# Local values of two runs as one operation on four tiles of TensorE, and narrow products split into 32 columns

## The chip, the cores and the metric

The kernel runs on one core of one Trainium2 chip. The metric is the device time of one execution in microseconds (us). It was run three times before the change: 905.56, 905.9 and 907.25 us, the median is 905.9 us.

## The reference

Attention with 4 batches, 8 heads, 576 tokens and head size 64, followed by two feed-forward layers on 2304 tokens of width 512 with inner width 2048. All is fp32. Cut to what matters:

```python
q_d, k_d, v_d = (x.reshape(B, H, S // 4, 4, D).mean(axis=3) for x in (q, k, v))
out_up = np.repeat(softmax(q_d @ k_d.T / 8) @ v_d, 4, axis=2)       # pooled over four tokens
mask = np.abs(pos[:, None] - pos[None, :]) < 4
out_local = softmax(np.where(mask, q @ k.T / 8, -1e9)) @ v          # seven neighbours
x = (out_up + out_local).transpose(0, 2, 1, 3).reshape(2304, 512)
h = x @ w_in;  x = np.where(h > 0, h, np.exp(np.minimum(h, 0)) - 1) @ w_out
h = x @ w2_in; out = (s * np.maximum(h, 0) ** 2 + b) @ w2_out
```

## The kernel before, in words

Attention is worked in units: one batch and one pair of heads (16 units, `hp` is the pair). A unit has a pooled part and a local part.

The pooled part: `tr` (L678) transposes q and k on TensorE, copies them to SBUF as `T` (scaled for q) and sums groups of four tokens out of PSUM with a reduction on VectorE (L689) to give `d`. `gs` (L702) multiplies the sums to pooled scores: for each head a matmul that loads 72 columns (a half of 144 pooled queries) and moves 144 pooled keys. After a softmax `gpt_` (L748) transposes the weights, and `gpv` (L767) multiplies with the summed values `vd`: for each head and half of the keys a matmul that loads 64 columns and moves 72 or 144.

The local part exists so in the first two batches alone (`DIRECT = 2`; the other two work it on VectorE and GpSimd in `direct`). The tokens of a half (288) are nine blocks of 32 queries; a block sees 38 keys. `ls` (L788) makes the scores of both heads, 18 matmuls that load 32 columns and move 38, into a PSUM tile for each head. `softmax` (L810) leaves weights for both heads in one buffer `p`; `lpt_` (L853) transposes it, so that head 0 stands on partitions 0 to 37 and head 1 on 64 to 101. `lpv` (L866) multiplies with the windows of v: 18 matmuls that load 64 columns (38 rows) and move 32, head 0 in the first 64 rows and 64 columns of the array, head 1 in the last, into one PSUM tile. Its result and the pooled one are added (L880), split into a high and a low fp32r part (`split`, L897) and used as input of the first feed-forward layer, or stored for later.

The first batch runs in two stages: `attention0` with the first half of the tokens before any feed-forward product, `attention0_rest` with the second half beside the first products. The second batch (`attention`) runs both halves of each unit beside feed-forward products. `ffn_h` (L1040) and `ffn_x` (L1086) are the first layer, with 256 columns moved by each matmul; lines 1474, 1502 and 1572 the second layer, which the change does not touch.

The order on every engine comes from a planner. Each operation is given an engine, an estimated duration, what it reads and writes, and a due time; `Plan.emit` runs a simulated clock over all of them and issues, for each engine, the ready operation with the earliest due time. A hand-tuned table `SHIFT` adds or takes away from the due times of operations by their number. Where TensorE would be idle in the plan `fill` puts in matmuls of zeros (L1635, source `wz`); before an operation that is not feed-forward, up to the planned time `DENSE_TILL`, `thicken` puts some in too when the planned feed-forward work just before it is below `DENSE`. Loads go through SP's queue, with a planned transfer time of bytes times `slow`. PSUM has three rings of tiles: `at` (2), `h` (2) and `acc` (4); a ring's next tile waits until its last user is done. Softmax buffers `p` are two, `pt` three.

Of the kernel before, what the change touches and what calls it, by code (L numbers as in the profile page):

```python
# [99 lines left out]
class Plan:  # L100
# [11 lines left out]
    SHIFT = ((29, 33, -0.5), (124, 125, 4.5), (127, 131, -22), (172, 178, -5), (212, 218, 11), (220, 226, 17.5),  # L112
# [9 lines left out]
    ENTER = 4.0  # L122
    DENSE = 0.9
    DENSE_TILL = 45.0
# [226 lines left out]
def attn_moe_moe2(ctx, tc, q, k, v, w_in, w_out, w2_in, w2_out, s2, b2, mask, mask_d, out):  # L351
# [32 lines left out]
    for tag, n, size in (("raw", 2, 8192), ("ev", 2, 2048), ("xr", 2, 2048), ("r", 2, 1024), ("wu", 2, 3584), ("pt", 3, 1152),  # L384
                         ("p", NLP, 1536), ("gnm", 2, 16), ("lmx", 2, 24), ("lrs", 2, 24), ("gs4", 2, 16), ("grs", 2, 16),
                         ("dmx", 2, 16), ("dsm", 2, 16)):
        ar.place(tag, n, size, "work")
# [29 lines left out]
             "lsm": [p1.tile([QB, 2 * NQB, 2], F32, name=f"lsm{i}") for i in range(2)],  # L417
# [69 lines left out]
    def weights(ph, f):  # L487
# [9 lines left out]
        for i in range(2):  # L497
# [9 lines left out]
            load(rawp[i], 524288, ld, due - RL, u=[raw])  # L507
# [37 lines left out]
    class Unit:  # L545
        def __init__(self, b, hp):
# [38 lines left out]
            self.gp, self.gpt, self.lp, self.lpt = {}, {}, {}, {}  # L585

# [5 lines left out]
        def loads(self, due, late=0, nb=0.0, nb_late=0.0):  # L592
# [9 lines left out]
            def parts(i, n0, n1, late):  # L602
                for a in range(2):
# [3 lines left out]
                         due + (late if late else 0), u=[self.nat], slow=1.2, nb=nb + (nb_late if late else 0), queue=e)  # L607
# [13 lines left out]
            load(self.vg, 294912, vg, due + VO, u=self.both if b == 0 else (), nb=nb)  # L621

            def vw(half, a):

                n, o = NQB * CT, a * D
                at = (2 * hp + a + b * H) * S + half * HS - 3
                dst = self.vw(half)
# [8 lines left out]
            def loads_v(half):  # L636
                for a in range(2):
                    load(self.vwp[half], VR * NQB * CT * 256, lambda a=a: vw(half, a),
                         due + VO + (late if half else 0), r=[self.vd] if b == 0 and half else (), u=self.both,
                         n=3 if (b, hp, a, half) == (0, 0, 0, 0) else 1, slow=1.2, nb=nb + (nb_late if half else 0))  # L640
# [37 lines left out]
        def tr(self, i, half, due):  # L678
            ps = self.ps([128, NQB, QB])

            def pe():
                for m in range(NQB):
# [5 lines left out]
                 scale=SCALE if i else 1.0, r=[ps], w=[self.T], u=self.tdv, due=due)  # L688
# [13 lines left out]
        def gs(self, heads, halves, due):  # L702
# [998 lines left out]
```

## Time and profile before

| what | value |
|---|---|
| median of three runs | 905.9 us (905.56 to 907.25) |
| the profiled execution, its own time | 906.92 us |
| its span, first to last instruction | 905.1 us |
| TensorE busy, weight loads busy | 893.3 us, 863.2 us |
| VectorE, ScalarE, GpSimd busy | 703.0, 546.6, 385.3 us |
| mean granted TensorE clock | 0.994 of full |

A busy share says how long an engine had an instruction under way. TensorE's instructions overlap, and the ends of its matmuls are modelled, so the time that a group of them takes is better read from the start of the group to the start of the next. In a timeline, equal instructions that follow each other are one row with their count.

### The profile page before, as it was taken

To read this page: it belongs to the slowest core of one execution; us is meant where nothing else is said; L and a number is where in the kernel's file an instruction comes from. 1 tells how busy PE (TensorE), PEld (TensorE's weight loads), DVE (VectorE), ACT (ScalarE), POOL (GpSimd) and SP (SyncE) were. 2 spreads that over 40 slices of the span, in tenths; PEclk is the share of its full clock that TensorE was granted. 3 is DMA by queue.
4 is the path that set the end of the run, shared out by engine and by line. 5 is a ranking of instruction groups with operands and counts; after the bars stand their busy time and mean duration, and the time that the engine had idled before them with its cause. 6 is when DMAs were issued, how large, how long until landed. Compare 5 with 4: busy or idle time off the path is not lost.

```text
span 905.1 us, 21207 instructions
## 1 busy us (share of the span) xinstructions
PE 893.3 (99%) x8417; PEld 863.2 (95%) x8417; DVE 703.0 (78%) x1090; ACT 546.6 (60%) x1175; POOL 385.3 (43%) x349
## 2 busy tenths in 40 slices
PE   9999999999999999999999999999999999999998
PEld 5678999999999989999999999999999999999998
DVE  5467766798888888889775768999836999677785
ACT  6587767565445545444566675656665887566642
POOL 3656557687887877988536664000000000000000
PEclk9989999999999999999999999999999999999999
DMA  9839676563353453343502156699963884353411
GB/s 188 221 116 237 187 184 172 132 175 92 90 135 80 106 130 105 85 114 101 158 7 94 49 188 215 239 335 342 362 217 120 271 296 150 110 180 104 157 37 35
DMA packets 123524, 142.88 MB, mean 158 GB/s; under 512 B 50976, under 2 KB 93984, under 8 KB 123424
## 3 DMA queue, kind: packets, MB, share of 16 engines
q1 hardware_dynamic: 121632, 141.07, 52.5%
q8 instruction: 66, 1.08, 0.5%
q10 hardware_dynamic: 1792, 0.44, 0.2%
q14 instruction: 34, 0.28, 0.1%
HBM read 101.12 MB, written 40.37 MB: 156 GB/s over the span
## 4 chain that ended last, share of the span: by engine, by line
PE 92%; DVE 2%; DMA 2%; POOL 1%; ACT 1%; issue 1%; SPq 1%; POOLq 0%; ACTq 0%
PE acc L1086 21%; PE h L1040 18%; PE acc L1572 11%; PE acc L1502 10%; PE h L1572 6%; PE h L1502 5%; PE at L1572 3%; PE acc L1040 3%; PE at L1502 3%; PE acc L1474 3%; DMA work<-in_moe_w_out_dram 1%; PE at L874 1%; PE at L775 1%; PE at L1635 1%; PE at L683 1%
## 5 line engine op out<-in xcount | busy, mean ns | idle before, releaser
L1086 PE MATMUL acc<-split,w 128*128 128x256 f32 x1728 | 234.4, 286 | 0.0
L1086 PEld LDWEIGHTS acc<-split,w 128*128 128x128 f32 x1728 | 217.2, 190 | 2.2 <-issue 1.7
L1040 PE MATMUL h<-split,w 128*128 128x256 f32 x1488 | 201.4, 286 | 1.6 <-POOL split L465 1.3
L1040 PEld LDWEIGHTS h<-split,w 128*128 128x128 f32 x1488 | 186.6, 189 | 4.1 <-POOL split L465 1.5
L465 POOL TENSOR_TENSOR split<-work,split 128x256 fp32r<-128x256 f32 (+1 forms) x148 | 138.6, 947 | 71.6 <-ACT split L457 54.9
L1572 PE MATMUL acc<-w,attn 128*128 128x256 f32 x864 | 106.1, 281 | 0.0
L1572 PEld LDWEIGHTS acc<-w,attn 128*128 128x128 f32 x864 | 104.1, 189 | 0.0
L1502 PE MATMUL acc<-attn,w 128*128 128x256 f32 x768 | 99.3, 282 | 0.0
L1502 PEld LDWEIGHTS acc<-attn,w 128*128 128x128 f32 x768 | 95.3, 188 | 0.0
L457 ACT ACTIVATE split<-work 128x256 fp32r<-128x256 f32 (+2 forms) x164 | 67.3, 422 | 45.0 <-DVE work L1064 26.9
L1064 DVE SCALAR_TENSOR_TENSOR work<-work,h 128x256 f32<-128x256 f32 x124 | 50.9, 415 | 55.4 <-ACT work L1062 55.2
L1060 ACT ACTIVATE work<-h 128x256 f32<-128x256 f32 x124 | 46.9, 379 | 75.4 <-PE h L1040 48.7
L465 POOL TENSOR_TENSOR work<-work 128x896 f32<-128x896 f32 (+1 forms) x42 | 69.1, 1652 | 15.9 <-DVE work L847 7.6
L1564 DVE TENSOR_TENSOR attn<-split,attn 128x1024 fp32r<-128x1024 f32 x43 | 52.6, 1223 | 21.5 <-ACT attn L1563 21.1
L1563 ACT ACTIVATE attn<-split 128x1024 fp32r<-128x1024 f32 x43 | 45.2, 1056 | 32.5 <-DVE split L1583 13.9
L982 DVE TENSOR_REDUCE work<-work 128x128 f32<-128x896 f32 x36 | 63.5, 1790 | 1.6 <-POOL work L465 1.6
L1062 ACT ACTIVATE work<-work 128x256 f32<-128x256 f32 x144 | 59.8, 417 | 4.0
L1572 PE MATMUL h<-w,attn 128*128 128x256 f32 x432 | 54.2, 281 | 0.0
L1522 ACT ACTIVATE split<-split 128x512 f32<-128x512 f32 x44 | 27.5, 629 | 41.4 <-DVE split L1512 40.6
L1572 PEld LDWEIGHTS h<-w,attn 128*128 128x128 f32 x432 | 52.5, 189 | 0.0
L1502 PE MATMUL h<-attn,w 128*128 128x256 f32 x384 | 51.2, 282 | 0.0
L1502 PEld LDWEIGHTS h<-attn,w 128*128 128x128 f32 x384 | 48.3, 188 | 0.0
(192 smaller groups left out, 1535.6 us busy)
## 6 DMA issues: line engine op xcount, KB each, us to landing
gd<-split SPq DMA_DIRECT2D x57, 256.0 KB
work<-gd SPq DMA_DIRECT2D x20, 512.0 KB
work<-in_moe_w_in_dram SPq DMA_DIRECT2D x16, 512.0 KB
work<-in_moe_w_out_dram SPq DMA_DIRECT2D x16, 512.0 KB
work<-in_moe_w_in_dram SPq DMA_DIRECT2D x8, 1024.0 KB
work<-in_moe_w_out_dram SPq DMA_DIRECT2D x8, 1024.0 KB
split<-gd SPq DMA_DIRECT2D x16, 512.0 KB
work<-in_k_dram SPq DMA_DIRECT2D x17, 320.0 KB
```

What stands on the lines that cost most here:

```text
L457: a = ((0.07 if first.slot in plan.spare else 0.11) + n / 1200, lambda: nc.scalar.activation(out=out(), in_=src(), func=ACTF.Copy, scale=s ...
L465: f = lambda e: lambda: e.tensor_tensor(out=out(), in0=in0(), in1=in1(), op=alu)
L982: op("dve", 0.07 + 14 * D / 546, lambda: nc.vector.tensor_reduce(out=vo()[:, WD + j * D:WD + (j + 2) * D].rearrange("p (j d) -> p j d", j= ...
L1040: nc.tensor.matmul(ps(), lhsT=w()[:, wpart, 0, c * 128:(c + 1) * 128], rhs=x.at(xpart)[:, c, :], start=first and i == 0, stop=last and i = ...
L1060: op("act", ta + 0.095, lambda: nc.scalar.activation(out=e(), in_=ps(), func=ACTF.Relu, scale=-1.0), r=[ps], w=[r1], u=[e], due=due)
L1062: op("act", ta, lambda: nc.scalar.activation(out=e(), in_=e(), func=ACTF.Exp, scale=-1.0), r=[r1], w=[r2], u=[e], due=due)
L1064: op("dve", td, lambda: nc.vector.scalar_tensor_tensor(out=e(), in0=e(), scalar=-1.0, in1=ps(), op0=ALU.add, op1=ALU.max), r=[r2, ps], w=[ ...
L1086: nc.tensor.matmul(acc()[:, c * N:(c + 1) * N], lhsT=wo[:, cc * 128:(cc + 1) * 128], rhs=g(), start=first and c == 0, stop=end and c == 1)
L1502: nc.tensor.matmul(ps[:, q * 256:(q + 1) * 256], lhsT=factor(0, w[2 * u + q], i, wi, c), rhs=x[i]()[:, xi].rearrange("p (c t) -> p c t", c ...
L1563: act(lambda: nc.scalar.activation(out=f()[:, 0], in_=src(), func=ACTF.Copy), 1024, r=r, w=[hi], u=[f, src], due=e + 2 * k * PP)
L1564: on(lambda eng: eng.tensor_tensor(out=f()[:, 1], in0=src(), in1=f()[:, 0].bitcast(F32), op=ALU.subtract), 1024, ("dve", "pool"), r=[*r, h ...
L1572: nc.tensor.matmul(m[i]()[:, c * 256:(c + 1) * 256], lhsT=f()[:, xi, o:o + 128], rhs=factor(1, w[pair], i, wi, 0), start=qd == 0 and p == ...
```

## The change

Three things change in what is computed where. (1) Local values: a `Pair` takes two runs, each a unit's half, and keeps for each head one buffer `p` with both runs in it, so that after the transposes run 0 stands on partitions 0 to 37 and run 1 on 64 to 101. The runs are the second halves of two neighbouring units in the first batch, and both halves of a unit in the second batch. The windows of v are loaded to partitions by run instead of by head. The values of both runs are one operation of 36 matmuls on four tiles: rows by run, columns by head, each run with its own PSUM tile. (2) Pooled scores, pooled values and those local values that stay single (first half of the first batch) issue each matmul as pieces of 32 columns. (3) The sums over four tokens read the copy in SBUF, and wait for it; the scale of the pooled scores changes with it.

The planner gets other numbers too: shorter estimates for the split products, another `SHIFT` table, `DENSE` 1.0 instead of 0.9 and `DENSE_TILL` 100 instead of 45, other `slow` factors of loads (w_in 1.05, w_out 0.74 instead of 1; q, k and windows of v 1.38 instead of 1.2; v in groups 1.1 instead of 1). The maxima, sums and their ring get four buffers instead of two. In the second half of the first batch all four units' local exponentials go to ScalarE with sums (before, three did). There the late loads of v's windows for two units are issued after the pooled products of the second.

```diff
     def tr(self, i, half, due):
...
-            op("dve", 0.38, lambda: nc.vector.tensor_reduce(
-                out=self.d()[:, i, half * G:(half + 1) * G], in_=ps().rearrange("p n (i r) -> p (n i) r", r=4),
-                axis=AX.X, op=ALU.add), r=[ps], w=[self.d], u=self.tdv, due=due)
+            op("dve", 0.38, lambda: nc.vector.tensor_reduce(
+                out=self.d()[:, i, half * G:(half + 1) * G], in_=self.T()[:, i, half * HS:(half + 1) * HS].rearrange("p (i r) -> p i r", r=4),
+                axis=AX.X, op=ALU.add), r=[copied], w=[self.d], u=[*self.tdv, self.T], due=due)
...
     def gs(self, heads, halves, due):
...
-                        nc.tensor.matmul(ps()[:, i, :], lhsT=self.d()[a * D:(a + 1) * D, 1, half * G:(half + 1) * G],
-                                         rhs=self.d()[a * D:(a + 1) * D, 0, :], start=True, stop=True)
+                        for c in range(0, G, 32):
+                            q0, q1 = half * G + c, half * G + min(c + 32, G)
+                            nc.tensor.matmul(ps()[c:min(c + 32, G), i, :], lhsT=self.d()[a * D:(a + 1) * D, 1, q0:q1],
+                                             rhs=self.d()[a * D:(a + 1) * D, 0, :], start=True, stop=True)
...
     def gpv(self, halves, due):
...
-                        nc.tensor.matmul(ps()[a * D:(a + 1) * D, :], lhsT=self.vd()[:, 2 * a + kc, :],
-                                         rhs=pt[a][0]()[:, pt[a][1], kc, :], start=(kc == 0), stop=(kc == 1))
+                        for c in range(0, D, 32):
+                            nc.tensor.matmul(ps()[a * D + c:a * D + c + 32, :], lhsT=self.vd()[:, 2 * a + kc, c:c + 32],
+                                             rhs=pt[a][0]()[:, pt[a][1], kc, :], start=(kc == 0), stop=(kc == 1))
...
     def lpv(self, half, due):
...
-                        nc.tensor.matmul(ps()[o:o + D, i * SB:(i + 1) * SB], lhsT=self.vw(half)[o:o + SW, i],
-                                         rhs=pt[o:o + SW, i * SB:(i + 1) * SB], start=True, stop=True)
+                        for c in (o, o + 32):
+                            nc.tensor.matmul(ps()[c:c + 32, i * SB:(i + 1) * SB], lhsT=self.vw(half)[o:o + SW, i, c - o:c - o + 32],
+                                             rhs=pt[o:o + SW, i * SB:(i + 1) * SB], start=True, stop=True)
...
+    class Pair:
...
+        def values(self, due):
+            pss = [u.ps([128, HS], how) for (u, _), how in zip(self.runs, ('at', 'at'))]
+            at = [[u.win(half, a) for a in range(2)] for u, half in self.runs]
+            def pe():
+                for i in range(NQB * CT):
+                    for r, a in ((0, 0), (1, 1), (0, 1), (1, 0)):
+                        v, o = at[r][a][:2]
+                        nc.tensor.matmul(pss[r]()[a * D:(a + 1) * D, i * SB:(i + 1) * SB], lhsT=v()[o:o + SW, i],
+                                         rhs=self.pt[a]()[o:o + SW, i * SB:(i + 1) * SB], start=True, stop=True)
...
+    pairs = [Pair((units[i], 1), (units[i + 1], 1)) for i in range(0, HP, 2)]
...
     def attention0_rest():
...
-            u.gpv(second, d), u.lpv(1, d)
+            u.gpv(second, d)
+            if u.hp % 2:
+                pairs[u.hp // 2].values(d)
...
     def attention(b):
...
+        local = [Pair((u, 0), (u, 1)) for u in us]
...
+            u.gs((0,), both, d(hp, 2)), u.gs((1,), both, d(hp, 3)), pr.part(0, d(hp, 4)), pr.part(1, d(hp, 5))
+            u.gpt_((0,), both, d(hp, 6)), u.gpt_((1,), both, d(hp, 7)), pr.finish(0, d(hp, 8)), pr.finish(1, d(hp, 9))
+            u.gpv(both, d(hp, 10)), pr.values(d(hp, 11))
```

## Rows read from the trace of the kernel before

**Rows 1.** The page: busy us of each engine (share, instructions), and the chain by engine.

```profile
PE 893.3 (99%) x8417; PEld 863.2 (95%) x8417; DVE 703.0 (78%) x1090; ACT 546.6 (60%) x1175; POOL 385.3 (43%) x349
...
PE 92%; DVE 2%; DMA 2%; POOL 1%; ACT 1%; issue 1%; SPq 1%; POOLq 0%; ACTq 0%
```

**Rows 2.** Busy time by stage: stretch, its length, engines' busy us, PEclk, DMA, GB/s.

```profile
34.00:84.00 50.00, 45.12 (x586) 37.27 (x585) 28.93 (x69) 36.16 (x112) 28.81 (x32) 0.93 0.63 171
84.00:150.00 66.00, 65.61 (x860) 62.30 (x859) 45.37 (x103) 49.93 (x123) 42.96 (x42) 1.00 0.72 189
150.00:460.00 310.00, 308.18 (x2800) 301.24 (x2800) 258.70 (x415) 159.66 (x462) 238.22 (x205) 0.99 0.44 115
```

**Rows 3.** TensorE's groups by shape: line, out<-in, rows*columns loaded, moved, count, busy, mean ns.

```profile
L874 PE MATMUL at<-work,attn 38*64 38x32 f32 x288 | 9.9, 220 | 0.0
...
L802 PE MATMUL at<-attn 64*32 64x38 f32 x256 | 4.0, 199 | 0.0
```

**Rows 4.** Timeline of TensorE, 112 to 126 us: start, length, line, what, count.

```profile
112.00 0.72 PE L710 MATMUL at<-attn 64*72 64x144 f32 x8
112.65 1.70 PE L1086 MATMUL acc<-split,w 128*128 128x256 f32 x12
...
120.28 0.72 PE L775 MATMUL at<-work,attn 72*64 72x144 f32 x8
120.93 1.24 PE L874 MATMUL at<-work,attn 38*64 38x32 f32 x36
122.10 2.66 PE L1040 MATMUL h<-split,w 128*128 128x256 f32 x20
...
124.79 0.54 PE L802 MATMUL at<-attn 64*32 64x38 f32 x36
125.25 0.73 PE L1040 MATMUL h<-split,w 128*128 128x256 f32 x4
```

**Rows 5.** The same timeline, 67 to 70 us: pooled products of the first batch.

```profile
67.71 0.47 PE L710 MATMUL acc<-w 64*72 64x144 f32 x4
...
69.27 0.48 PE L775 MATMUL at<-work,w 72*64 72x72 f32 x8
```

**Rows 6.** VectorE's groups: busy us, mean ns, idle time before them, by releaser.

```profile
L689 DVE TENSOR_REDUCE w<-at 128x72 f32<-128x288 f32 x16 | 7.0, 453 | 6.8 <-PE at L683 4.7 <-ACT w L457 2.0
L689 DVE TENSOR_REDUCE attn<-at 128x72 f32<-128x288 f32 x16 | 7.0, 450 | 1.0 <-PE at L683 0.6 <-ACT attn L457 0.4
```

**Rows 7.** Timeline of TensorE, 46 to 84 us; in brackets its idle time before.

```profile
46.78 0.57 PE L795 MATMUL acc<-msk,identb 96*96 96x114 bf16 x2 [2.72 <-ACT attn L732]
...
50.07 2.08 PE L1040 MATMUL h<-split,w 128*128 128x256 f32 x8
...
58.72 1.19 PE L1040 MATMUL h<-split,w 128*128 128x256 f32 x8
...
82.72 1.34 PE L1040 MATMUL h<-split,w 128*128 128x256 f32 x9 [1.31 <-POOL split L465]
```

**Rows 8.** Busy time in two stretches at half clock, columns as in rows 2.

```profile
48.80:55.60 6.80, 6.70 (x32) 4.58 (x31) 2.37 (x8) 4.76 (x20) 3.58 (x4) 0.50 0.51 150
325.30:328.70 3.40, 3.40 (x17) 3.18 (x15) 3.40 (x5) 1.65 (x5) 1.59 (x2) 0.50 0.15 39
```

**Rows 9.** The chain of waits, 36 to 84 us: start, length, what.

```profile
37.98 6.72 DMA work<-in_moe_w_out_dram
...
73.20 5.92 DMA attn<-in_v_dram
```

**Rows 10.** Timeline of TensorE at 324 us.

```profile
324.68 0.41 PE L758 MATMUL at<-ident,attn 72*72 72x72 f32 x4 [1.82 <-DVE attn L465]
```

**Rows 11.** Timeline of all engines, 78 to 83 us: from a local value to its split.

```profile
78.09 0.46 DVE L880 TENSOR_TENSOR attn<-at,attn 128x288 f32<-128x288 f32 x1 [0.87 <-ACT w L457]
...
78.58 0.39 ACT L457 ACTIVATE split<-attn 128x224 fp32r<-128x224 f32 x1 [0.21 <-DVE attn L880]
...
81.57 1.10 POOL L465 TENSOR_TENSOR split<-attn,split 128x224 fp32r<-128x224 f32 x1
```

More of the change, by code (lines that the diff above doesn't have):

```diff
@@ L416, in attn_moe_moe2 @@
     rings = {"gsm": [p1.tile([G, 2, 2], F32, name=f"gsm{i}") for i in range(2)],
-             "lsm": [p1.tile([QB, 2 * NQB, 2], F32, name=f"lsm{i}") for i in range(2)],
+             "lsm": [p1.tile([QB, 2 * NQB, 2], F32, name=f"lsm{i}") for i in range(4)],
              "ds": [p1.tile([128, 4, 8], F32, name=f"ds{i}") for i in range(2)]}
@@ L585, in __init__, with win @@
             self.gp, self.gpt, self.lp, self.lpt = {}, {}, {}, {}
+            self.pairs = {}
+        def win(self, half, a):
+            if half not in self.pairs:
+                return lambda: self.vw(half), a * D, self.both, [self.vd]
+            pr = self.pairs[half]
+            r = pr.runs.index((self, half))
+            if self.b:
+                return lambda: self.vw(a), r * D, self.both, []
+            home = pr.runs[a][0]
+            return lambda: home.vw(half), r * D, home.both, [home.vd]
         def ps(self, shape, how="at"):
@@ L606, in parts @@
                          lambda a=a, e=e: nat(i, n0, n1, a, nc.scalar if e == "act" else nc.sync),
[L607 removed]
+                         due + (late if late else 0), u=[self.nat], slow=1.38, nb=nb + (nb_late if late else 0), queue=e)
             parts(0, 0, 2 * NQB, 0)
@@ L619, in vg @@
                     in_=v[b, 2 * hp:2 * hp + 2].rearrange("a (h i r) d -> i (a h) (r d)", h=2, r=4))
-            load(self.vg, 294912, vg, due + VO, u=self.both if b == 0 else (), nb=nb)
+            load(self.vg, 294912, vg, due + VO, u=self.both if b == 0 else (), slow=1.1, nb=nb)
             def vw(half, a):
-                n, o = NQB * CT, a * D
+                n = NQB * CT
                 at = (2 * hp + a + b * H) * S + half * HS - 3
-                dst = self.vw(half)
+                dst, o = self.win(half, a)[:2]
+                dst = dst()
                 if at < 0:
@@ L638, in loads_v @@
                     load(self.vwp[half], VR * NQB * CT * 256, lambda a=a: vw(half, a),
-                         due + VO + (late if half else 0), r=[self.vd] if b == 0 and half else (), u=self.both,
-                         n=3 if (b, hp, a, half) == (0, 0, 0, 0) else 1, slow=1.2, nb=nb + (nb_late if half else 0))
+                         due + VO + (late if half else 0), r=self.win(half, a)[3] if b == 0 and half else (), u=self.win(half, a)[2],
+                         n=3 if (b, hp, a, half) == (0, 0, 0, 0) else 1, slow=1.38, nb=nb + (nb_late if half else 0))
             loads_v(0)
@@ L788, in ls, with ls_products @@
         def ls(self, half, due):
+            self.softmax(self.ls_products(half, due), half, due)
+        def ls_products(self, half, due):
             F = NQB
@@ L807, in ls @@
             op("pe", 0.66, pe, r=[self.T, c_msk], w=pss, u=self.tdv, due=due, tail=-0.09)
-            self.softmax(pss, half, due)
+            return pss
         def softmax(self, pss, half, due):
@@ L1153, in Bs @@
             u.gs((0, 1), first, d), u.ls(0, d), u.vsum(d + VP)
-            u.loads_late()
+            if (u.hp % 2):
+                for x in units[u.hp - 1:u.hp + 1]:
+                    x.loads_late()
         def C(u, d):
@@ L1174, in Bs @@
         def Bs(u, d):
-            u.gs((0, 1), second, d), u.ls(1, d)
+            u.gs((0, 1), second, d), pairs[u.hp // 2].part(u.hp % 2, d)
         def C(u, d):
-            u.gpt_((0, 1), second, d), u.lpt_(1, d)
+            u.gpt_((0, 1), second, d)
+            for a in range(2 * (u.hp % 2)):
+                pairs[u.hp // 2].finish(a, d)
         def Dd(u, d):
-            u.gpv(second, d), u.lpv(1, d)
+            u.gpv(second, d)
+            if u.hp % 2:
+                pairs[u.hp // 2].values(d)
         n = HP
```

91 lines of the change are left out of this document (74 added, 17 removed), and 17 rows, old and new, of the table SHIFT.

## The prediction

> **What bounds the kernel now.** I read the page's busy shares first, then its chain of waits, then busy time by stage, then TensorE's groups by shape, and last the order of time around the touched products. TensorE is busy 893.3 of 905.1 us, and 92% of the chain that ended last is its own work [rows 1]. No other engine is near that. By stage, from 84 us to 460 us it idles 0.39 + 1.82 us in 376 [rows 2], so there a microsecond less of TensorE work is a microsecond less of time. Two stages differ. Before 34 us attention of the first batch waits for loads and softmax, and the planner fills the gaps with idle products of zeros. From 34 to 84 us, where the second half of the first batch runs beside the first products of the feed-forward layer, TensorE idles 4.88 us and its granted clock is 0.93 of full [rows 2].
>
> So the question is what the touched products occupy of TensorE, and whether the new order opens or closes gaps between 34 and 84 us. A product's recorded length includes a modelled end, so I take an operation as lasting until the next one starts. Each fp32 matmul runs as two instructions (the second batch's eight local value operations of 18 matmuls are the 288 of [rows 3]); counts below are of instructions.
>
> **Part 1: local values on four tiles.** Now one half of one head pair is 36 instructions from 120.93 to 122.10 us, 1.17 us or 32.5 ns each [rows 4]. They alternate between two tiles of 64 columns: head 0 on the first 64 rows and columns of the array, head 1 on the last. There are 16 such operations. The change leaves four of them (first batch, first half) alone and joins twelve into six, of 72 instructions each, going round four tiles. The trace of before has no operation on four tiles of 64 columns. Bounds: at the pace of two tiles a pair takes 72 x 32.5 = 2.34 us, the gain is 0; nothing makes it dearer, since number, width and alternation of tiles stay. At the pace of the local scores, on six tiles of 32 columns, 36 instructions from 124.79 to 125.25 us [rows 4], 12.8 ns each, a pair takes 0.92 us and gains 1.42. Between them I argue by tile: 32.5 ns on two tiles is 65 ns for each tile's own instruction, 12.8 ns on six is 77 ns. The pace goes about with the number of tiles, though widths differ little in one and much in the other. Four tiles then take 16.2 to 19.2 ns an instruction, 1.17 to 1.38 us a pair. I take 1.25: 1.09 us less, six times, **6.5 us**, all in stages where TensorE is the bound or nearly so. The ends, 0 and 8.5 us, stay for the range.
>
> Both row halves now write one PSUM tile [rows 3]; the new operation gives each row half a tile of its own. The Trainium skill (TensorEngine Tiling (Array Packing), Restrictions and Gotchas) says that different row tiles cannot use the same PSUM bank at the same time. By that rule the two tiles of before never ran together and the new ones can, two at a time: half the pace time, 1.17 us a pair, 7.0 us in all and a total 0.5 us lower. It is a reason for the four tiles; no row of before shows two 64-column tiles overlapping, which is why the end at 0 keeps a chance of its own.
>
> **Part 2: 32 columns at a time.** Pooled scores: for the later three batches 12 blocks of two adjacent operations; one takes 112.00 to 112.65 us, 0.65 us for 8 instructions [rows 4]. Each matmul becomes three (32 + 32 + 8 columns), all moving the same 144 columns. Pooled values: 12 operations, 120.28 to 120.93 us, 0.65 us [rows 4], each matmul becoming two. Bounds: if split tiles run one after another, 1.95 and 1.30 us; if they overlap fully, and the two heads as well, about 0.33 each. The nearest row with 32-column tiles is the local scores: three column tiles of the same row half next to each other at 12.8 ns an instruction, so three of them go through in 77 ns while one 64-column matmul of similar movement takes 65 [rows 4]. So splitting costs little, and the head that follows can start in other columns before the one ahead is done. I take one step in four saved less overhead, 0.52 us: 24 x 0.13 = **3.1 us**. In the first batch the recorded lengths are 0.47 and 0.48 us [rows 5], eight of each; the eight that lie after 34 us save an estimated 0.1 us each by the same share, **0.8 us**, the eight before 34 us nothing, since idle products fill what they leave. The same holds for the four local value operations of the first half, from 1.17 to somewhere between 0.92 and 2.34 us: idle products cover it, and only the last before the feed-forward start would show.
>
> The Trainium skill (TensorE: Matmul & The Clock Gate, Part 3: Packing small matmuls, The mechanism) says that a weight load overlaps a running matmul only when its row group differs. The three pieces of a pooled score share a row group, so by that rule they would go in series, and it speaks against this part; the local scores, three column tiles in one row group at 12.8 ns, disagree with it [rows 4]. What it would give is the last rival below.
>
> **Part 3: what changes off TensorE.** The sums over four tokens are 32 reductions of 0.45 us, which now read the SBUF copy. Their length I keep. They wait for the copy, 0.4 us, and TensorE's pooled scores wait for them; DVE's own later work queues behind. In the trace part of their idle time already ends with that copy on ScalarE [rows 6], so bound 0 to 0.8 us at the start, and I take 0. The PSUM tile is freed sooner, which the gaps hide. In the first batch the second half of unit 3 moves its exponentials from one ScalarE instruction after DVE to six with sums: some 3 us more on ScalarE, which is busy 36.16 of 50 us in that stage [rows 2]; covered, at worst its share of a gap. The late value loads of a pair are issued together on SP's queue, after the pooled sum of both units, ahead of or behind weight loads; bytes and count are the same.
>
> **Part 4: the new order.** The stage from 34 to 84 us loses in four ways. TensorE idles 2.72 us before 46.78 and 1.31 us before 82.72 [rows 7], and the first is followed by 6.8 us at half clock (1.2 of 2.4 GHz), 48.8 to 55.6 [rows 8], in which eight instructions of the feed-forward layer take 2.08 us instead of 1.19 [rows 7]; at half pace 6.8 us lose 3.4. Both gaps lead back to transfers on the chain of waits, a weight load of 6.72 us and one of v of 5.92 us [rows 9]. The change plans with other load times (1.38 instead of 1.2 times their bytes for q, k and the windows of v, 0.74 for w_out) and goes on filling with idle products until 100 us of planned time instead of 45, up to 1.0 instead of 0.9 us per stretch. That can remove up to 2.72 + 1.31 + 3.4 = 7.4 us; the added idle products cost TensorE time where nothing idles. A later gap, 1.82 us before 324.68 with 3.4 us at half clock after it (half of that, 1.7, lost) [rows 8, 10], hangs on the same table of shifted due times, and can go or come again elsewhere. From -3 (a new gap as large) to +10.9 us; I take **1.4 us** gained, the half clock after 48.8 mended and about 2 us of idle products paid for it.
>
> **The sum.** 6.5 + 3.1 + 0.8 + 1.4 = 11.8 us. The profiled execution took 906.92 us, its span 905.1, and 1.8 us lie outside, which do not change. 906.92 - 11.8 = 895.1; that execution is 1.0 us above the median of the runs, 905.9, so I predict 894.1 us.
>
> **The rivals.**
> - *Two tiles' pace stays* (0.20). The local values gain nothing, as the only row with 64-column tiles would have it. 894.1 + 6.5 = 900.6 us.
> - *Pairing starves TensorE at 80 us* (0.10). The values of units 2 and 3 now come together, after the softmax of the later one. Behind them stand the same sum of 0.46 us, copy, and subtraction of 1.10 us on GpSimd [rows 11] a second time, some 1.95 us with a copy of 0.39, before the second block of tokens may begin; the gap there grows from 1.31 to 3.3 us, longer than the 2.72 that cost a half clock of 3.4 us. 894.1 + 1.95 + 3.4 = 899.4 us. For it: GpSimd is already what TensorE waits for at 82.72. Against: the first token block has more work that could fill.
> - *All gaps close* (0.08). 905.9 - 10.4 - 10.9 = 884.6 us.
> - *Split tiles run in series* (0.08), the one that ends slower. Pooled scores cost 3 x 0.65, pooled values 2 x 0.65: 12 x 1.30 + 12 x 0.65 = 23.4 us more, and in the first batch 4 x 2 x 0.47 + 4 x 0.48 = 5.7 more. 905.9 - 6.5 - 1.4 + 29.1 = 927.1 us. It decides from the point where a late block costs 0.33 us more than now (24 x 0.33 = 7.9). Against it stands the pace of the local scores; for it, that those move 38 columns and these 144.
>
> **How the numbers follow.** The forecast has 0.54. Its own range, with the ends of part 1 near its estimate and part 4 within 4 us, is 889 to 899. For 8 in 10 it has to reach the first two rivals and some way toward closed gaps: 886.5 to 903.5 us. A measurement here tells 0.2%, some 1.8 us, from no change. Faster by more than that: the forecast, closed gaps, and the two rivals near 900 except where they come with other losses, 0.85. Within 0.2%: 0.06, from those. Slower: the series, and a little for a worse order, 0.09.
>
> **What would show it.** Right: six value operations of 72 instructions lasting 1.2 to 1.4 us each; a block of pooled scores and a pooled value operation at about 0.5 us; no half clock between 45 and 60 us; TensorE without idle time from 84 us on. Wrong: value operations of 2.3 us (first rival); a gap of 3 us or more near 80 us (second); pooled scores above 0.98 us (last). The prediction fails altogether if the new order opens gaps of more than 10 us together.

## The result and the profile after

The change made the kernel slower: 916.33 us (median of 4 runs, 912.0 to 920.15) against 905.73 us (4 runs of the kernel before beside them), a ratio of 1.0129 [1.0094, 1.0164]; the two medians by themselves give 1.0117, which lies inside. The prediction was 894.1 us, range 886.5 to 903.5. The profiled execution of after took 916.17 us, its span is 914.4 us, 9.3 more than before.

The page of after, busy time and the chain by engine, against [rows 1]:

```profile
PE 900.9 (99%) x9029; PEld 862.5 (94%) x9029; DVE 704.7 (77%) x1089; ACT 545.2 (60%) x1185; POOL 390.0 (43%) x351
...
PE 89%; DVE 4%; DMA 2%; ACT 2%; issue 2%; POOL 2%; SPq 0%; DVEq 0%; POOLq 0%; ACTq 0%
```

Busy time by stage of after, columns as in [rows 2]:

```profile
0.00:34.00 34.00, 30.42 (x581) 17.54 (x581) 16.96 (x54) 19.28 (x84) 14.81 (x35) 0.93 0.96 208
34.00:84.00 50.00, 48.99 (x777) 36.85 (x776) 30.86 (x72) 38.21 (x126) 28.18 (x30) 0.98 0.65 159
84.00:150.00 66.00, 63.63 (x937) 59.29 (x941) 47.77 (x106) 47.08 (x121) 43.86 (x44) 0.95 0.69 182
150.00:460.00 310.00, 306.60 (x2979) 298.66 (x2973) 263.70 (x418) 156.98 (x457) 233.71 (x197) 0.99 0.44 116
```

From 34 to 84 us TensorE now idles 1.01 us instead of 4.88, as forecast. But the clock fell before 34 us, where it had not, and from 84 to 150 us the idle time rose from 0.39 to 2.37 us and the clock fell to 0.95.

The values on four tiles did what was said. In the timeline of TensorE one operation of 72 instructions lasts 80.61 - 79.43 = 1.18 us (1.25 was said), and the pooled values behind it 121.69 - 121.05 = 0.64 us, the pooled scores 157.16 - 156.51 = 0.65 us, as long as whole ones in [rows 4]:

```profile
79.43 1.25 PE L999 MATMUL at<-work,w 38*64 38x32 f32 x72
80.61 0.98 PE L1196 MATMUL acc<-split,w 128*128 128x256 f32 x6
...
121.05 0.71 PE L790 MATMUL at<-work,attn 72*32 72x144 f32 x16
121.69 0.98 PE L1196 MATMUL acc<-split,w 128*128 128x256 f32 x6
...
156.51 0.72 PE L724 MATMUL at<-attn 64*32 64x144 f32 x24
157.16 0.98 PE L1196 MATMUL acc<-split,w 128*128 128x256 f32 x6
```

What ate the gain shows in three views. First, the same timeline where TensorE waits for "issue", that is for nothing the profile shows, in the middle of an operation:

```profile
28.91 0.48 PE L820 MATMUL acc<-w 64*32 64x35 f32 x22
30.87 0.30 PE L820 MATMUL acc<-w 64*32 64x38 f32 x14 [1.47 <-issue]
...
122.60 1.25 PE L999 MATMUL at<-work,attn 38*64 38x32 f32 x71
125.53 0.31 PE L999 MATMUL at<-work,attn 38*64 38x32 f32 x1 [1.69 <-issue]
```

Before has no such wait. The DMA packets of the trace name a candidate: queue q8 brings instructions, 16 KB at a time, and one such packet is under way from 27.8 to 29.3 us, another from 123.1 to 124.1, just as TensorE runs dry (at 29.4 and 123.8 us). The last section follows this up.

Second, four stretches at half clock, 20.4 us together (before 10.2, [rows 8]); half of the difference, 5.1 us, is lost:

```profile
26.10:29.50 3.40, 3.29 (x63) 1.98 (x52) 0.76 (x3) 1.78 (x8) 1.56 (x3) 0.50 1.14 273
32.90:36.30 3.40, 3.40 (x60) 1.40 (x49) 2.71 (x6) 1.81 (x6) 0.84 (x1) 0.50 0.52 118
125.10:131.90 6.80, 6.37 (x29) 6.31 (x30) 4.33 (x4) 1.97 (x2) 4.02 (x4) 0.50 0.60 149
176.30:183.10 6.80, 6.80 (x93) 6.74 (x86) 3.42 (x10) 1.73 (x4) 0.74 (x1) 0.50 0.36 119
```

The second and the third come after the two waits for issue; the first begins before them. The last follows a wait that the timeline of all engines explains. VectorE sums k and q for 4.5 us, a feed-forward step (L1174) stands behind that, ScalarE waits for the step, and a copy behind it on ScalarE's queue holds up the local values:

```profile
169.51 3.12 DVE L674 TENSOR_TENSOR attn<-attn 72x512 f32<-72x512 f32 x1
...
172.66 1.39 DVE L676 TENSOR_TENSOR attn<-attn 72x256 f32<-72x256 f32 x1
...
173.98 0.41 DVE L1174 SCALAR_TENSOR_TENSOR work<-work,h 128x256 f32<-128x256 f32 x1
...
174.42 0.42 ACT L456 ACTIVATE split<-work 128x256 fp32r<-128x256 f32 x1 [3.67 <-DVE work L1174]
...
175.91 2.19 PE L999 MATMUL at<-work,attn 38*64 38x32 f32 x72 [2.34 <-ACT work L456]
```

Third, the idle products, in TensorE's groups; of before:

```profile
L1635 PE MATMUL at<-wz 128*128 128x512 bf16 (+1 forms) x48 | 12.7, 391 | 1.0 <-DVE wz L1640 1.0
...
L1635 PE MATMUL h<-wz 128*128 128x512 bf16 (+1 forms) x33 | 7.3, 331 | 0.0
...
L1635 PE MATMUL acc<-wz 128*128 128x512 bf16 (+1 forms) x20 | 4.2, 341 | 0.0
```

and of after:

```profile
L1753 PE MATMUL at<-wz 128*128 128x512 bf16 (+1 forms) x94 | 25.0, 393 | 1.0 <-DVE wz L1758 1.0
...
L1753 PE MATMUL h<-wz 128*128 128x512 bf16 (+1 forms) x29 | 6.2, 326 | 0.0
...
L1753 PE MATMUL acc<-wz 128*128 128x512 bf16 (+1 forms) x30 | 5.4, 306 | 0.0
```

101 became 153. Counted to the start of the next instruction they take 21.6 us before and 31.8 after: 15.1 to 19.0 us before the first feed-forward product, 6.5 to 10.9 from there to 84 us, 0 to 2.0 later.

So the books of the two traces: local values -6.9 us (18.7 to 11.8, of which the pairs 14.0 to 8.5), pooled products 0.0 (22.5 in both, the scores 0.4 less and the values 0.4 more), idle products +10.2, idle time of TensorE +1.6 (7.8 to 9.4), half clock +5.1. The sum, +10.0, is near the 9.3 by which the span grew; what ran at half clock is in part counted twice. The sum says what TensorE did, not what caused it; an idle product may stand in a wait. That took experiments.

### The profile page after: what moved, and what is told of

It is laid out like the page before. It is cut to its first block, busy times and chain, and to the rows that moved or that the text cites. A ratio compares the mean times of both kernels' runs of the same rounds, so it can differ in the third digit from the quotient of the medians.

```text
span 914.4 us, 22464 instructions
## 1 busy us (share of the span) xinstructions
PE 900.9 (99%) x9029; PEld 862.5 (94%) x9029; DVE 704.7 (77%) x1089; ACT 545.2 (60%) x1185; POOL 390.0 (43%) x351
## 4 chain that ended last, share of the span: by engine, by line
PE 89%; DVE 4%; DMA 2%; ACT 2%; issue 2%; POOL 2%; SPq 0%; DVEq 0%; POOLq 0%; ACTq 0%
PE acc L1196 21%; PE h L1150 18%; PE acc L1690 11%; PE acc L1620 10%; PE h L1690 6%; PE h L1620 5%; PE acc L1150 3%; PE at L1690 3%; PE at L1620 3%; PE acc L1592 3%; PE at L1753 1%; DMA attn<-in_v_dram 1%; POOL w L464 1%; DMA work<-in_moe_w_out_dram 1%; DVE work L516 1%
## 5 line engine op out<-in xcount | busy, mean ns | idle before, releaser
L1196 PE MATMUL acc<-split,w 128*128 128x256 f32 x1728 | 237.5, 287 | 0.0
L1196 PEld LDWEIGHTS acc<-split,w 128*128 128x128 f32 x1728 | 219.6, 191 | 3.8 <-issue 3.4
L1150 PE MATMUL h<-split,w 128*128 128x256 f32 x1488 | 203.7, 286 | 1.4 <-DVE work L1174 0.5
L464 POOL TENSOR_TENSOR split<-work,split 128x256 fp32r<-128x256 f32 (+2 forms) x143 | 127.7, 902 | 76.8 <-ACT split L456 65.0
L1174 DVE SCALAR_TENSOR_TENSOR work<-work,h 128x256 f32<-128x256 f32 x124 | 50.8, 415 | 49.5 <-ACT work L1172 49.0
L464 POOL TENSOR_TENSOR work<-work 128x896 f32<-128x896 f32 (+1 forms) x46 | 77.2, 1691 | 20.2 <-DVE work L1092 8.6
L1682 POOL TENSOR_TENSOR attn<-split,attn 128x1024 fp32r<-128x1024 f32 x1 | 3.2, 3232 | 189.9 <-ACT attn L1681 189.9
L1453 POOL TENSOR_TENSOR w<-work,w 128x1024 fp32r<-128x1024 f32 x16 | 39.4, 2463 | 21.2 <-ACT w L1452 21.1
```

Of the source, the lines that this page charges most:

```text
L464: f = lambda e: lambda: e.tensor_tensor(out=out(), in0=in0(), in1=in1(), op=alu)
L1150: nc.tensor.matmul(ps(), lhsT=w()[:, wpart, 0, c * 128:(c + 1) * 128], rhs=x.at(xpart)[:, c, :], start=first and i == 0, stop=last and i = ...
L1174: op("dve", td, lambda: nc.vector.scalar_tensor_tensor(out=e(), in0=e(), scalar=-1.0, in1=ps(), op0=ALU.add, op1=ALU.max), r=[r2, ps], w=[ ...
L1196: nc.tensor.matmul(acc()[:, c * N:(c + 1) * N], lhsT=wo[:, cc * 128:(cc + 1) * 128], rhs=g(), start=first and c == 0, stop=end and c == 1)
L1682: on(lambda eng: eng.tensor_tensor(out=f()[:, 1], in0=src(), in1=f()[:, 0].bitcast(F32), op=ALU.subtract), 1024, ("dve", "pool"), r=[*r, h ...
```

## The experiments

Theory O: the new order (shifted due times, load factors, idle products) gave the gain away. Theory S: the pieces of 32 columns did, through waits for instructions. Most kernels below keep the order of every operation and change only what one operation issues; so only that differs, and with the number of TensorE's instructions the places where its 16 KB packets begin. Ratios are to before, on the same chip (its medians there were 904.0 to 905.8 us).

| kernel | us | ratio [95%] | first feed-forward product, us |
|---|---|---|---|
| before | 905.73 | 1 | 34.0 |
| after | 916.33 | 1.0129 [1.0094, 1.0164] | 40.1 |
| b_split | 904.81 | 0.9994 [0.9971, 1.0017] | 36.1 |
| a_unsplit | 913.12 | 1.0097 [1.0070, 1.0125] | 39.4 |
| b_noshift | 918.9 | 1.0162 [1.0135, 1.0189] | 38.7 |
| a_noshift | 916.54 | 1.0125 [1.0092, 1.0158] | 41.3 |
| a_nofill | 912.01 | 1.0075 [1.0046, 1.0103] | 42.5 |
| a_first | 915.27 | 1.0130 [1.0097, 1.0163] | 42.9 |
| a_two | 917.13 | 1.0154 [1.0111, 1.0198] | 42.4 |
| b_lpv | 901.44 | 0.9975 [0.9956, 0.9995] | 35.0 |
| b_lpv, again | 899.7 | 0.9958 [0.9934, 0.9982] | 35.5 |
| b_lpv_nofill | 903.6 | 0.9997 [0.9972, 1.0023] | 35.3 |
| a_tuned | 906.06 | 1.0033 [1.0006, 1.0059] | 35.3 |
| a_tuned_psum | 904.06 | 0.9995 [0.9975, 1.0015] | 39.3 |
| a_plain | 908.36 | 1.0045 [1.0026, 1.0063] | 36.0 |
| a_late | 909.03 | 1.0052 [1.0029, 1.0075] | 36.6 |
| b_early | 902.32 | 0.9983 [0.9960, 1.0005] | 41.1 |
| a_late_tr | 905.03 | 1.0002 [0.9970, 1.0033] | 36.1 |

**Pieces in before, pieces undone in after.** b_split gives before the pieces in pooled scores, pooled values and all local values; a_unsplit takes them from after's pooled products.

```diff
-  nc.tensor.matmul(ps()[o:o + D, ...], lhsT=self.vw(half)[o:o + SW, i], rhs=pt[...])
+  for c in (o, o + 32):
+      nc.tensor.matmul(ps()[c:c + 32, ...], lhsT=self.vw(half)[o:o + SW, i, c - o:c - o + 32], rhs=pt[...])
```

> The kernel before with its order of instructions unchanged; only the pooled scores, pooled values and all 16 local value operations are issued in pieces of 32 columns. Theory O (the new order of work costs the time, the new products are harmless or cheaper): 898 to 906 us; the split local values last about 0.85 us instead of 1.17, the pooled products keep 0.65 us. Theory S (the split products themselves cost it, by more instructions that TensorE must fetch): 908 us or more, with idle time inside operations that no wait explains.

> The changed kernel with its order unchanged, but pooled scores and pooled values are not split (local values stay as changed). Theory O: 912 to 920 us, no better than the changed kernel, start of the first feed-forward product still near 40 us. Theory S: 910 us or less, and the unexplained idle time inside operations near 29 and 124 us is gone.

b_split is level with before, although a late local value operation fell from 1.17 to 0.8 us; its timeline has a wait of 2.61 us for issue inside the local scores, from 24.9 to 27.5 us, and one of 1.24 later:

```profile
24.51 0.40 PE L805 MATMUL acc<-w 64*32 64x35 f32 x29
27.51 0.27 PE L805 MATMUL acc<-w 64*32 64x38 f32 x7 [2.61 <-issue]
```

a_unsplit came 0.3% below after, which is within the intervals; it still waits 2.6 us for issue at 29.2 us and 1.2 at 65.0, though not at 124. Both came out as O said, and the order of after looked like the larger cause. That holds only while the local values of the first half stay in pieces, as a_plain shows below.

**Without the tables of shifted due times.** In b_noshift and a_noshift `SHIFT = ()`.

> The kernel before with an empty table of shifted due times. Both theories: slower than before, some 915 to 930 us; it is the base for the next run.

> The changed kernel with an empty table of shifted due times. Theory O (what the change saves on TensorE is there, and the hand-tuned table of before was worth more than that of after): 5 to 12 us faster than the kernel before with an empty table. Theory S: as slow as it or slower.

Before's table is worth 13 us on the chip, after's nothing. With empty tables the change as a whole gains 2.4 us, less than the 5 to 12 that O forecast and not clear of noise (the intervals overlap). A table that suits the chip is worth more than that; this speaks for O, but two orders differ in too many things to say more.

**Idle products, and the first of them.** a_nofill issues none from 34 us of planned time on; a_first cuts those ahead of the first transposes.

```diff
-                self.keep_warm(best[1], idle, t0 < 1)
+                if t1 - idle < 34.0:                                    # a_nofill, and so in thicken
+                    self.keep_warm(best[1], idle, t0 < 1)
...
+                self.keep_warm(best[1], idle - 2.6 * (t0 < 1), t0 < 1)  # a_first
```

> The kernel after in its own order on every engine, without the idle products (zeros) that it issues from the planned start of the feed-forward layer on (from 34 us); in the trace of after these take 12.9 us of TensorE, 10.9 of them before 84 us; in that of before 6.5 us. Theory O (the new order costs the time, and its idle products occupy TensorE where nothing makes it wait): the first layer starts at the same time, about 40 us, and the whole comes out 8 to 12 us earlier, 904 to 908 us. Rival O2 (the idle products lie in true waits, for the softmax of a pair, a load, a copy): idle time of TensorE between 40 and 84 us grows by about as much as the products took, no gain, 914 to 917 us, or up to 3 us more where a stretch at half clock follows the longer waits. Rival S (the splits cost the time by making TensorE wait for its own instructions): no change either, 914 to 917, but idle time does not grow.

> The kernel after in its own order, with the idle products ahead of its very first real product cut from 20 to as many as planned time less 2.6 us gives (about 14, as before has). In the trace of after the first transposes begin at 7.11 us, in before at 5.22, behind 6.28 against 4.39 us of idle products; the planner made the stretch longer because it reckons the loads of q and k at 1.38 instead of 1.2 times their bytes. Theory O: if the transposes wait for nothing but the idle products, they begin up to 1.9 us earlier, the first feed-forward product too (38 instead of 39.9), and the whole is 914 to 915 us. Rival: the start is set by later loads and by softmax, the 1.9 us are lost again before the first feed-forward product, 916 us. A third way: with fewer idle products the clock falls early; then 917 to 920.

a_nofill came out 5 us below after, between O and O2, and the gain is not where the products stood: its trace lacks the wait for issue at 123.8 us and the half clock behind it. Its stage from 34 to 84 us idles 6.64 us, at a clock of 0.84:

```profile
34.00:84.00 50.00, 43.36 (x753) 33.37 (x754) 29.83 (x69) 36.28 (x123) 25.46 (x29) 0.84 0.58 149
```

From the first to the 145th feed-forward product after takes 44.2 us, a_nofill 45.7. So there O2 holds: the products lie in true waits. a_first moved nothing either: what it begins earlier is lost before the first feed-forward product. Its profiled execution was the slowest of its four, 919.35 us.

**Two tiles at a time.** a_two issues the same 72 instructions of a value operation, two tiles after the other two.

```diff
-                for i in range(NQB * CT):
-                    for r, a in ((0, 0), (1, 1), (0, 1), (1, 0)):
+                for two in (((0, 0), (1, 1)), ((0, 1), (1, 0))):
+                    for i, (r, a) in ((i, x) for i in range(NQB * CT) for x in two):
```

> The kernel after in its own order; the six value operations go through the same 72 instructions on the same tiles and PSUM tiles, but first those of two tiles (upper rows with left columns, lower rows with right columns), then those of the other two. If the pace comes from the number of tiles in use, each lasts about 2.3 us instead of 1.25 (32.5 ns an instruction as in before), and the whole is some 6 us longer, 921 to 923. If it comes from the two PSUM tiles alone (before wrote one), the pace stays near 17 ns and the time at 916. Part 1 of the prediction says the first.

```profile
81.42 2.09 PE L999 MATMUL at<-work,w 38*64 38x32 f32 x72
83.44 0.74 PE L1196 MATMUL acc<-split,w 128*128 128x256 f32 x4
```

83.44 - 81.42 = 2.02 us, 28 ns an instruction (2.3 us was expected by the number of tiles alone). Before, two tiles into one PSUM tile took 32.5 ns, four take 16.4. So the number of tiles makes the pace, and a PSUM tile of its own for each row half makes a seventh at most. The Trainium skill (TensorEngine Tiling (Array Packing), Restrictions and Gotchas) says that row tiles cannot write one PSUM bank at the same time, by which two tiles with a PSUM tile each, if in different banks, should have taken half the time of before; this trace does not bear that out. The whole is not measurably slower than after (1.0154 against 1.0129, intervals overlap), although TensorE has 0.84 us more to do six times. That is no clean test of what TensorE's time is worth there: the wait in the fourth value operation (1.69 us in after) is 0.21 us here, as TensorE comes later to the same instruction, and its idle time in all is 7.9 us instead of 9.4.

**The late local values alone.** b_lpv gives before pieces of 32 columns in the twelve local value operations beside feed-forward products and nowhere else; b_lpv_nofill also issues no idle products from 34 us on.

```diff
+                        n = 32 if self.b or half else D
+                        for c in range(o, o + D, n):
```

> The kernel before in its own order, with the local values alone in pieces of 32 columns, and of these only the twelve operations that run beside feed-forward products (second half of the first batch, whole second batch). In the trace with all products split such an operation took about 0.8 us instead of 1.17. Theory S (splits are good, unless many small instructions come close together at the start and TensorE runs ahead of its own instructions): 12 x 0.35 = 4.2 us less, no wait for instructions near 25 to 30 us, 901 to 902.5 us. Theory O (nothing but order and chance of the clock matters at this size): within 1 us of before, 905 to 906.5.

> The kernel before in its own order with the twelve late local value operations in pieces of 32 columns (901.4 us), and without the idle products from 34 us on, which take 6.0 us there. If they lie in true waits, no gain: 901 to 903 us; if the longer waits then bring the half clock between 45 and 60 us, 903 to 906; if they take TensorE time of their own, 895 to 898.

b_lpv is the one version measurably faster than both kernels, 901.44 us, and 899.7 when it was run again. An operation lasts 117.44 - 116.69 = 0.75 us, 10.4 ns an instruction:

```profile
116.69 0.82 PE L876 MATMUL at<-work,attn 38*32 38x32 f32 x72
117.44 1.82 PE L1042 MATMUL h<-split,w 128*128 128x256 f32 x13
```

Twelve save 12 x (1.17 - 0.75) = 5.0 us of TensorE, and 2 to 4 us come out. S expected this. Without the idle products no gain is left to measure (0.9997): its trace has 17.1 us at half clock, those of b_lpv 6.8 and 0, as the second of its three forecasts said.

**All pieces undone, or the early ones alone.** a_plain takes after's pieces away everywhere, a_late in the first batch alone (`n = 32 if self.b else ...`), b_early gives before those of the four local value operations before 34 us alone.

> The kernel after in its own order on every engine, with all pieces of 32 columns undone: pooled scores, pooled values and the four single local value operations of the first half. Theory S (the many small instructions up to 33 us make TensorE wait for its next instructions, and the clock falls): no wait of over 1 us for instructions before the first feed-forward product, that product at 36 to 38 us instead of 39.9, the time 909 to 912. Theory O (the order makes the first batch late): first product at 39 to 40 us, 912 to 914 us, as with the pooled products alone undone (913.1).

> The kernel after in its own order on every engine, with the pieces of 32 columns undone in the first batch alone (pooled products and single local values); the later batches keep theirs. Theory S (only the many small instructions close together at the start cost, by a wait for instructions and the clock behind it): as with all pieces undone, 907 to 910 us, the first feed-forward product at 35 to 37 us, no wait of over 1 us for instructions before it. Rival L (the pieces cost wherever they stand, in the later batches by their number): 912 to 915 us.

> The kernel before in its own order, with pieces of 32 columns in the four single local value operations of the first half alone, all before 34 us; each is 0.3 to 0.4 us shorter for it. Theory S: the pieces bring a wait of 1 to 3 us for instructions between 24 and 31 us, the first feed-forward product comes 1 to 3 us later than 33.8 us, and the time is 906 to 909 us, slower than before although TensorE has less work. Rival (that wait needs the pooled pieces too, or the other order): no such wait, the time of before within 1 us.

a_plain and a_late agree: 8 and 7 us of after's time hung on the pieces at its start, nothing on those of the later batches; rival L fell. Neither has a wait for issue of over 0.5 us. But only a part of the 7 to 8 us is lost at the start. Against after, the first feed-forward product comes 4.1 us earlier in a_plain and 3.5 in a_late, the 300th (111.9 us in after) 0.5 and 2.7, the 400th (135.0) 5.2 and 7.1. Between these two lies after's wait at 123.8 us with 6.8 us at half clock behind it. It stands in the values on four tiles, which both kernels issue unchanged, and there it is gone, in a_late:

```profile
119.86 1.25 PE L1000 MATMUL at<-work,attn 38*64 38x32 f32 x72
121.04 2.78 PE L1197 MATMUL acc<-split,w 128*128 128x256 f32 x18
```

So the pieces at the start cost most of it far behind themselves. What changes there is how many instructions came before, and with it where a packet falls (last section). That this part of the loss is the packets' place alone is inferred, not tested by itself. Over all kernels the line is sharp: TensorE's waits for issue sum to 2.7 to 5.6 us in the eight that have pieces in the first half's local values (after, a_unsplit, a_noshift, a_nofill, a_first, a_two, b_split, b_early) and to 0 to 1.1 us in the others.

b_early shows the mechanism and refutes the price that S gave it. Its timeline of TensorE:

```profile
24.65 0.39 PE L876 MATMUL h<-work,w 38*32 38x32 f32 x24
27.48 0.86 PE L876 MATMUL h<-work,w 38*32 38x32 f32 x48 [2.44 <-issue]
...
41.06 1.20 PE L1042 MATMUL h<-split,w 128*128 128x256 f32 x8
...
60.70 0.47 PE L710 MATMUL acc<-w 64*72 64x144 f32 x4
```

and the stretch behind the wait, at half clock for 13.6 us:

```profile
27.00:40.60 13.60, 13.12 (x275) 8.51 (x276) 5.81 (x15) 5.86 (x13) 6.13 (x7) 0.51 0.66 122
```

The first feed-forward product comes 7 us late (1 to 3 were forecast), yet the pooled scores that before starts at 59.84 us start at 60.70, 0.9 us late, and the whole is no slower. In before's order the stage behind absorbs a late start. In after's order it does not, up to there: from the first to the 145th feed-forward product pass 43.5 to 45.7 us in after, a_unsplit, a_nofill, a_first, a_two, a_plain and a_late, whether the first comes at 36.0 or at 42.9 us. In before, b_split, b_early and b_lpv (both times) it is 40.6 to 46.8, least in b_early, which starts last. Which operation carries the delay in after's order was not settled.

**Another order.** a_tuned has after's structure with all pieces whole, before's planned durations for them, and a table found anew; a_tuned_psum also sums from PSUM again, with its own table.

> The kernel after with pooled scores, pooled values and single local values whole again and their planned durations as in before (values on four tiles 1.2 us), and with another table of shifted due times, so with another order on every engine. All else as in after: values on four tiles, sums from SBUF, load factors, idle products by the same rule. Theory O (what four tiles save is there, and it was the order of after that gave it away): the six value operations of 1.25 us stay, the order falls no worse than that of before, and the time is 897 to 904 us. Rival P (pairing, the sums' wait for the copy and the load factors make the first batch late in any order): the first feed-forward product again comes at 39 us or later (33.8 in before) and the time is 908 to 916 us.

> As a_tuned, but the sums over four tokens read PSUM as in before, with a table of its own found in the same way. If the sums' wait for the copy is what makes the first batch late (VectorE waits 5.9 us for that copy up to 40 us in after), the first feed-forward product comes 2 us or more before that of a_tuned and the time is 2 to 4 us below it. Theory O: no fixed difference, within 5 us of a_tuned either way, as orders differ.

Their profiled executions run at full clock throughout, and both come out near before, a_tuned 2 us above what O forecast and as far below what P did. So pairing, sums from SBUF and load factors do not force 916 us; but the 5.5 us that the pairs save show in the time of no order tried. With the sums from PSUM it is 2 us less, though the first feed-forward product comes 4 us later, not earlier: nothing here shows that the wait for the copy makes the start late, and 2 us is what two orders can differ by.

**One wait of after's order.** a_late_tr shortens the sums of k and q on VectorE, of which the one that matters here took 4.5 us in after and 2.6 in a_late. It leaves most of each sum out, so part of the pooled scores is not computed.

```diff
+                    w = 16 if e is nc.vector else D
-                    e.tensor_tensor(out=x[:, :, 0:2 * D], in0=x[:, :, 0:2 * D], in1=x[:, :, 2 * D:4 * D], op=ALU.add)
+                    e.tensor_tensor(out=x[:, :, 0:2 * w], in0=x[:, :, 0:2 * w], in1=x[:, :, 2 * D:2 * D + 2 * w], op=ALU.add)
```

> As a_late (after's order, no pieces in the first batch), and where VectorE sums rows of k or q of the last two batches (six times) it adds an eighth of the columns in one instruction and leaves the rest out, so that part of the pooled scores is not computed. In after that sum held VectorE for 4.5 us at 169.5 us, the feed-forward step behind it held ScalarE's queue for 3.67 us, and with it a copy that the local values wait for: TensorE idles 2.34 us there (3.3 in a_late) and then runs 6.8 us at half clock. If that wait is what the order of after loses in this stage: no idle time of over 1 us and no half clock between 160 and 185 us, 3.3 + 3.4 = 6.7 us less than a_late's 909.0, about 902.5 us. If other waits move up behind it: 905 to 909 us.

905.03 us, the low end of the second forecast: the wait fell from 3.3 to 2.0 us, the half clock from 6.8 to 3.4, which makes 3.0 us, and 4 to 4.5 us came back with all six sums shortened. What holds the same step now is mostly another addition on VectorE, 4.31 us long, with what is left of the sum behind it:

```profile
159.86 4.31 DVE L464 TENSOR_TENSOR split<-work,split 128x256 fp32r<-128x256 f32 x1
164.10 1.36 DVE L675 TENSOR_TENSOR attn<-attn 72x128 f32<-72x128 f32 x1
...
167.31 1.43 PE L1002 MATMUL at<-work,attn 38*64 38x32 f32 x72 [2.03 <-ACT work L456]
```

## Why the prediction was wrong

Forecast -11.8 us, measured +10.6.

- **Part 1, right.** Said 1.25 us a pair and 6.5 us in all; the trace has 1.18 to 1.31 us where nothing disturbs, and 5.5 us in the six pairs. The argument by tile held, and a_two shows that four tiles are the reason. But "all in stages where TensorE is the bound or nearly so" is not borne out: a_two spends 5 us more there and the time does not tell, though its waits shrank, and no order tried shows the 5.5 us.
- **Part 2, wrong: the step that failed first.** "I take one step in four saved less overhead, 0.52 us: 24 x 0.13 = 3.1 us." A late block stays at 0.64 to 0.65 us; the pieces neither overlap better nor go in series. The local scores at 12.8 ns, on which the step leaned, move 38 columns, these 144; I had written this difference down, for the rival alone. And pieces were priced by TensorE's pace alone. In the first half, "idle products cover it" was true of TensorE's work and not of its instructions: with pieces it gets through 256 of them in 2.7 to 5.6 us instead of 6.8 or more, before the next packet has come. Undoing the pieces there gave back 7 to 8 us (a_late, a_plain), most of it at the wait at 123.8 us that went with them; with the 3.1 + 0.8 forecast as gain it is some 11 of the 22 us between forecast and result.
- **Part 4, wrong.** "From -3 (a new gap as large) to +10.9 us; I take 1.4 us gained." The half clock at 48.8 us went, as taken. But the idle products cost 10.2 us of TensorE instead of about 2, and the order brought the wait at 173.6 us with 6.8 us at half clock; a_late_tr got back 4 to 4.5 us there, of which its trace shows 3.0. With pieces undone at the start and that wait eased, the change still stands level with before, not 6.5 us below: the idle products fill waits of the new order that before did not have (a_nofill). A table of due times had been priced as if it could only mend gaps that the trace shows.
- **Part 3**, taken as nothing, was not seen to cost at the start (a_tuned_psum).
- **The rivals.** The one that ended slower had the wrong mechanism: no series in the later batches. None named waits for instructions. The sign of failure "gaps of more than 10 us together" did not come, and the prediction failed without it: TensorE idles 9.4 us in after and 7.8 in before, and the clock costs 5.1 us more.

Open: why the 5.5 us of the pairs come out in no order, and what carries a late start through after's first stage up to 84 us.

## What to carry to other kernels

Price a split twice: by the engine's pace, and by how fast it then gets through its own instructions, above all where transfers already fill the DMA engines. Put it only where longer instructions surround it: the same pieces gained 2 to 4 us beside feed-forward products. A changed number of instructions also moves every later place where TensorE may wait for them, so look for idle time "issue" far behind the change too. When a change comes with a new order, test it with the order held fixed before crediting it; here the order alone was worth 13 us, more than the change.

## What was not expected of the hardware

TensorE can wait for its own instructions. The pages list the packets of queue q8 (queue, kind, packets, MB, share), of before and of after:

```profile
q8 instruction: 66, 1.08, 0.5%
...
q8 instruction: 71, 1.16, 0.6%
```

The traces record 16,952 and 18,180 instructions of TensorE (matmuls, weight loads and those of its sequencer), 257 and 256 to a packet. Counted so, all 19 waits for issue of over 0.35 us in the 18 traces come when 193 or 194 instructions and a multiple of 256 have started, and each ends 1.15 to 1.67 us after a packet has landed. So the place is fixed by the count, and the length by how late the packet is.

In after TensorE passes one such place at 117.0 us, the packet starts at 123.1, lands at 124.1, and TensorE, dry since 123.8, resumes at 125.5. In b_early it passes one at 20.1 us; the packet is under way from 24.9 to 25.9 us, and from 24.6 to 25.7 the loads take 103% of the DMA engines' time:

```profile
q1 hardware_dynamic: 301, 0.40, 103.0%
q8 instruction: 1, 0.02, 6.1%
```

TensorE stops at 25.0 and resumes at 27.5 us. Before is near the edge itself: it passes the place at 19.0 us, the packet lands at 24.4, and the next place comes at 25.9, 1.5 us later, with no wait. From one place to the next, in the first two steps that begin after 17 us, TensorE takes 6.8 to 10.2 us without its waits in the kernels that have no pieces in the first half's local values, and 2.7 to 5.6 in those that have (b_early 5.0, then 6.4). That the packet is the cause is inferred from these counts and times; it was not taken away by itself.

Width counts beside the number of tiles: four tiles of 64 columns go at 16.4 ns an instruction, four of 32 columns at 10.4 ns, and those with both row halves in one PSUM tile (b_lpv).
